# Column means of a weight matrix: four chunk sums side by side on the tensor engine's columns, and one product that adds them

## Chip, cores and metric

The kernel runs on one NeuronCore of a Trainium2 chip. The metric is the device time of one execution in microseconds (us), given as the median of several runs. Where the text names engines: PE is TensorE's matrix multiply, PEld its weight load, DVE is VectorE, ACT is ScalarE, POOL is GpSimd and SP is SyncE, which here only issues DMAs.

## What is computed

Attention with a hashed mask over 4 batches, 8 heads, 768 positions and head size 64, then a Fourier mixing layer and a two-layer MLP on the 4 x 768 x 512 result:

```python
mask = q_bucket[:, :, :, None] == k_bucket[:, :, None, :]     # 6 sign bits of q @ proj, k @ proj
scores = np.where(mask, scale * np.matmul(q, k.transpose(0, 1, 3, 2)), -1000000000.0)
attn = softmax(scores);  x = attn @ v, heads side by side      # (4, 768, 512)
mixed = np.real(np.fft.fft(np.fft.fft(x, axis=1), axis=2))
u = x + mixed
mu = np.mean(u, axis=-1, keepdims=True)
var = np.mean((u - mu) ** 2, axis=-1, keepdims=True)
un = (u - mu) / np.sqrt(var + 1e-06)
ch = np.maximum(un @ w_ch1, 0.0) @ w_ch2                       # 512 -> 2048 -> 512
return (u + ch).astype(np.float32)
```

Subtracting the mean of `u` over its 512 entries before the product with `w_ch1` is the same as subtracting from every column of `w_ch1` its mean over the 512 rows. The kernel does the latter, once, and the change is in how these column means are made. The two weight matrices come in as 64-bit floats and are narrowed to float32 on the core.

## The kernel before

**Stages.** `_main` runs batch by batch. `attention(b)` goes through four pairs of heads (`n`, 0 to 15 over the batches) and six chunks of 128 keys each (`c`). A step is one chunk: `weigh` makes scores for two halves of the queries (two PE groups, `sc`), ACT takes the exponential (`pk`, L860; there are two `pk` buffers), DVE adds the chunks up (`acc`, L944); `values` multiplies the chunk before by v (`oo`, L877). At the end of a pair, in the first step of the next one, `scale` sums over keys with a matrix of ones (`sum`, L897, two groups), and DVE transposes (L901), inverts and multiplies (L904 to L910). `prepare(n + 1)` transposes the next pair's q and k on DVE (L747) and makes their hash bits: for the pairs in `LITE` as `bitsq` and `bitsk` (L776, read by DVE at L778), for later pairs as `bits` (L791), four products of 32 columns each, written to the four groups of 32 partitions of one PSUM tile.

**What runs beside it.** In batch 0 each attention step is followed, in four steps out of five, by one step of `weights1()`: slice `i` of 16 slices of w1 (128 x 512 each, four row chunks `c` for each of four column blocks `f`) is narrowed by `convert(i)`: L631, L635 and L641 on DVE, L639, L646 and L647 on ACT, and a DMA for slice i + 7 issued by POOL. After the fourth slice of block 0, and again of block 512, `average(f)` and `centre(f, ...)` follow: four products with a 128 x 128 matrix `mean` whose entries are 1/512, accumulated in one PSUM tile (`wm`, L654), and four subtractions on DVE that read it from PSUM (L662). Blocks 1024 and 1536 are averaged after the last step of batch 0; ACT copies these two averages to SBUF (`mean`, L1442), and their eight subtractions are written after the second step of batch 1. From batch 1 on, `mix(b - 1)` runs beside attention: the folds (L994 to L1012, DVE), the channel transform (`cs`, L1034), the sequence transform (`A`, `B`, L1063), and the MLP. In batch 0's MLP, `quarters` (L1136 to L1142) makes sums of w1's quarters on DVE in one buffer (`tq`) and stores them to DRAM (`ad`) through the SP queue, where batches 1 to 3 fetch them.

**Order.** Batch 0's attention with `weights1` and the four averages stands in a block that keeps PE, DVE, ACT and POOL in the order in which the code is written (`manual_schedule`). The rest is ordered by a planner, which takes instructions by priority (by default the order in which they are written) and by when it reckons them ready. Every engine then works through its own list in order.

**PSUM.** During batch 0 to 2 `pt` hands out the two banks of the pool `ps_1` in turn; an averaging tile, the two `sum` tiles of `scale` and the bit tiles all go through these two.

Of the kernel before, what the change touches and what calls it, by code (L numbers as in the profile page):

```python
# [11 lines left out]
F32 = mybir.dt.float32  # L12
# [8 lines left out]
P = 128  # L21
B, H, S, D = 4, 8, 768, 64
NBITS = 6
DM = H * D
DFF = 4 * DM
# [5 lines left out]
NDC = DM // P  # L31
GTT = 2
GT = GTT * P
WC = 512
# [445 lines left out]
def _main(  # L480
# [13 lines left out]
    nc = tc.nc  # L494
# [13 lines left out]
    def wt(shape, dtype, tag, name, bufs=2):  # L508
        return work.tile(shape, dtype, tag=tag, name=name, bufs=bufs)
# [4 lines left out]
    def pt(shape, name):  # L514

        turn[0] += 1
        if roomy[0] and turn[0] % 2:
            if turn[0] % 4 == 1:
                return ps_o.tile(shape, F32, tag="o", name=name)
            return ps_sc.tile(shape, F32, tag="sc", name=name)  # L520
        return ps_1.tile(shape, F32, tag="ps", name=name)
# [14 lines left out]
    def load(n, names="qkv", second=nc.sync):  # L536

        b, t = divmod(n, NPAIR)
        for nm in names:
            src = {"q": q, "k": k, "v": v}[nm]
            tag, bufs = ("vn", 2) if nm == "v" else ("qkn", 2)
            tl = wt([P, S], F32, tag, f"{nm}n{n}", bufs)
            nat[nm, n] = tl
            if nm == "v" or n == 0:
                tc_ = tl.rearrange("p (c h d) -> p c h d", c=NT, h=2)
                for h in range(2):  # L550
                    s = src[b, 2 * t + h]
                    s = (
                        s.rearrange("(p c) d -> p c d", c=NT) if nm == "q"
                        else s.rearrange("(c p) d -> p c d", p=P)
                    )
                    (second if h else nc.sync).dma_start(tc_[:, :, h, :], s)
                continue
            for i in range(4):
                s = src[b, 2 * t + i // 2, :, i % 2 * 32 : i % 2 * 32 + 32]
                d = tl[32 * i : 32 * i + 32]  # L560
                if nm == "k":
                    nc.sync.dma_start(
                        d.rearrange("p (j a) -> p j a", a=32),
                        s.rearrange("(j b) a -> b j a", b=32),
                    )
                else:
                    s = s.rearrange("(j b r) a -> r b j a", b=32, r=2)
                    d = d.rearrange("p (r j a) -> r p j a", r=2, a=32)
                    for r in range(2):
                        nc.sync.dma_start(d[r], s[r])  # L570
# [23 lines left out]
    ones = const.tile([P, D], F32, tag="ones", name="ones")  # L594
# [12 lines left out]
    sq = const.tile([P, 2, 2, HALF + 1], F32, tag="sq", name="sq")  # L607
    ch = const.tile([P, 2, 2, DM // 2], F32, tag="ch", name="ch")
    mean = const.tile([P, P], F32, tag="mean", name="mean")
    nc.gpsimd.memset(mean, 1.0 / DM)  # L610
    w1 = const.tile([P, NDC, DFF], F32, tag="w1", name="w1")
    w2 = const.tile([P, NFC, DM], F32, tag="w2", name="w2")

# [35 lines left out]
        )  # L649

    def average(f):
        ps = pt([P, WC], f"wm{f}")
        for c in range(NDC):
            nc.tensor.matmul(  # L654
                ps, mean, w1[:, c, f : f + WC], start=(c == 0), stop=(c == NDC - 1)
            )
        return ps

    def centre(f, avg):
        for c in range(NDC):  # L660
            w = w1[:, c, f : f + WC]
            nc.vector.tensor_tensor(w, w, avg, op=ALU.subtract)  # L662
# [32 lines left out]
    def weights1():  # L695
        slices = [
            (w1[:, c, f : f + WC], moe_w_ch1[c * P : (c + 1) * P, f : f + WC])
            for f in range(0, DFF, WC)
            for c in range(NDC)
        ]  # L700
        zt = wt([P, 3, 2 * WC], F32, "z", "zraw1", 1)
        ft = wt([P, 12, WC], F32, "F", "fraw", 1)
        raws = [zt[:, i] for i in range(3)] + [
            ft[:, i : i + 2].rearrange("p i w -> p (i w)") for i in range(0, 8, 2)
        ]
        arrival = Arrival(slices, raws, 0)
        for i in range(arrival.depth):
            arrival.fetch(i, nc.sync)
            if i == 1:
                load(1)  # L710
        yield
        for i in range(len(slices)):
            arrival.convert(i, ft[:, 8 + i % 4].bitcast(I32))
            yield
            if i % NDC == NDC - 1:


                f = i // NDC * WC
                if f < DFF // 2:
                    centre(f, average(f))  # L720


    xs = {}
# [188 lines left out]
    def attention(b):  # L912
        xs[b] = wt([P, NPAIR, S], F32, "x", f"x{b}")
        pending = []

        def finish():
            n, c, pk, oos, sums = pending.pop(0)
            with behind() if n >= NPAIR and t is not None else nullcontext():
                values(n, c, pk, oos)
            if c == NT - 1:  # L920
                scale(n, oos, sums)

        for t in range(NPAIR):
            n = NPAIR * b + t
            half = fold(b, 0) if t == NPAIR - 1 else iter(())
            if 1 < n + 1 < NPAIR * B:
                load(n + 1)
            ahead = prepare(n + 1) if n + 1 < NPAIR * B else iter(())
            oos = [ps_o.tile([P, 512], F32, tag="o", name=f"oo{n}_{g}") for g in range(2)]
            acc = wt([P, 2, 2, HALF], F32, "t6", f"acc{n}", 2)  # L930
            first = None
            for c in range(NT):
                pk = weigh(n, c)
                new = pk[:, :, :, 0:HALF]
                sums = [acc]
                if c == 0:
                    first = new
                elif c == NT - 1 and b == 0:

                    sums.append(new)  # L940
                else:

                    for g in (0, 1) if b == 0 else (slice(0, 2),):
                        nc.vector.tensor_tensor(  # L944
                            acc[:, g], (first if c == 1 else acc)[:, g], new[:, g],
                            op=ALU.add,
                        )
                while pending:
                    finish()
                pending.append((n, c, pk, oos, sums))  # L950
                if c > 2:
                    next(half, None)
                if c > 0:
                    next(ahead, None)
                yield
        t = None
        while pending:
            finish()
# [459 lines left out]


    other = weights1()  # L1420
    next(other)
    nc.sync.dma_start(ch, cn["ch"].ap())
# [4 lines left out]
    with tc.manual_schedule(engines={ET.PE, ET.DVE, ET.Activation, ET.Pool}):  # L1427
        for _ in prepare(0):
            pass
        roomy[0] = False  # L1430
        for i, _ in enumerate(attention(0)):
            if i % 5 < 4:
                next(other, None)
        for _ in other:
            pass
        pwf = wt([P, 2, P], F32, "t6", "pwf", 2)
        nc.sync.dma_start(pwf, cn["pw"].ap())
        nc.scalar.copy(pw, pwf)
        means = []
        for f in range(DFF // 2, DFF, WC):  # L1440
            means.append((f, wt([P, WC], F32, "u", f"mean{f}", 2)))
            nc.scalar.copy(means[-1][1], average(f))  # L1442
    for b in range(B):
        if b > 0:

# [15 lines left out]
        if b == B - 1:  # L1461
# [7 lines left out]
            ps = pt([1, 3, P], "norms_t")  # L1469
# [25 lines left out]
def kernel(tc, *args):  # L1495

    cn = {n: tc.nc.inline_tensor(a, name="k_" + n) for n, a in _consts().items()}
    with ExitStack() as ctx:
        large = _main(ctx, tc, *args, cn)
    with tc.If(large > 0, preferred_fallthrough_block=False):  # L1500
        _any_scores(tc, *args, cn)
# [34 lines left out]
```

## Time and profile before

| what | value |
|---|---|
| median of 6 runs | 1115.57 us (1111.92 to 1118.81) |
| the profiled execution's own time | 1115.24 us |
| its span in the trace | 1113.5 us |
| mean granted TensorE clock | 0.994 |
| PE busy | 1070.1 us (96%) |
| DVE busy | 779.3 us (70%) |
| ACT busy | 453.5 us (41%) |
| the averages' products (L654) | 32 records, 35.5 to 135.5 us |

The page gives each engine's busy time over one execution. A float32 product shows as two PE records and two weight loads, so 16 products of the averages are 32 records. Successive records on PE overlap in the trace: what a group costs PE is the distance from its first start to the next group's start, not the sum of its durations. A number in brackets behind a row of the timeline is idle time of that engine before it and the instruction that ended it.

### The profile page before, as it was taken

The page shows a single profiled execution, that of the slowest core. Times are in us where ns is not written, and L with a number is a line of the kernel's source. Part 1 is how long each engine was busy: PE and PEld are TensorE (multiplying, and loading weights), DVE is VectorE, ACT ScalarE, POOL GpSimd, SP SyncE. Part 2 cuts the span into 40 slices and gives each one's busy share as a digit, 9 for nine tenths or more (in the row PEclk, how much of TensorE's full clock was granted, in tenths as well). Part 3 has the DMA queues.
Part 4 walks back from the last instruction along what each step waited for, and adds up shares of the span by engine and source line. Part 5 has one row for each costly group of instructions (what it writes and reads, how often), then busy time and mean ns, then how long its engine had stood idle before and what let it go on. Part 6 is the DMA issues. An engine that isn't in the chain of part 4 may idle for free.

```text
span 1113.5 us, 13886 instructions
## 1 busy us (share of the span) xinstructions
PE 1070.1 (96%) x4917; PEld 656.7 (59%) x4917; DVE 779.3 (70%) x1298; ACT 453.5 (41%) x875; POOL 79.5 (7%) x141
## 2 busy tenths in 40 slices
PE   7989998999999999999999999999999999999996
PEld 3434354455845576555664567645674569768675
DVE  5879978639589586985767796884866875644353
ACT  6768445525064224354325522354215422341420
POOL 1000000002110020030000011021000002100000
PEclk9999999999999999999999999999999999999998
DMA  9744544611056144223144234123032205122401
GB/s 227 198 96 100 95 134 141 214 35 26 1 132 209 43 101 141 43 67 82 29 147 94 68 67 165 32 46 95 20 110 71 73 32 170 48 86 73 135 19 41
DMA packets 175566, 103.13 MB, mean 93 GB/s; under 512 B 129408, under 2 KB 162816, under 8 KB 175488
## 3 DMA queue, kind: packets, MB, share of 16 engines
q1 hardware_dynamic: 168400, 83.93, 28.3%
q0 software_dynamic: 5520, 17.83, 5.1%
q8 instruction: 41, 0.67, 0.3%
q10 hardware_dynamic: 1568, 0.39, 0.2%
q14 instruction: 37, 0.30, 0.1%
HBM read 81.14 MB, written 20.97 MB: 92 GB/s over the span
## 4 chain that ended last, share of the span: by engine, by line
PE 63%; DVE 13%; ACT 2%; DMA 2%; issue 2%; DVEq 0%; ACTq 0%
PE o L1219 23%; PE h_p L1348 18%; PE h L1301 6%; PE sc L856 5%; PE oo L877 5%; DVE pk L866 4%; DVE acc L944 2%; PE cs L1034 2%; DMA zraw<-in_moe_w_ch_dram 2%; PE A L1063 1%; PE B L1063 1%; DVE x L1077 1%; PE sum L897 1%; ACT pk L860 1%; PE bits L791 1%
## 5 line engine op out<-in xcount | busy, mean ns | idle before, releaser
L1219 PE MATMUL o<-w,h 128*128 128x256 f32 x1152 | 258.9, 382 | 0.1
L1219 PEld LDWEIGHTS o<-w,h 128*128 128x128 f32 x1152 | 216.9, 190 | 42.4 <-issue 4.7
L860 ACT ACTIVATE pk<-sc 128x768 f32<-128x768 f32 x192 | 148.2, 808 | 98.9 <-PE sc L856 69.9
L866 DVE SCALAR_TENSOR_TENSOR pk<-qb,kb,pk 128x768 f32<-128x768 bf16 x132 | 128.7, 1013 | 64.7 <-ACT pk L860 61.9
L877 PE MATMUL oo<-pk,vn 128*64 128x385 f32 (+1 forms) x768 | 150.1, 500 | 5.2 <-DVE pk L866 2.6
L856 PE MATMUL sc<-qt,kt 64*128 64x384 f32 x768 | 152.5, 502 | 0.2 <-ACT pk L860 0.2
L1348 PE MATMUL h_p<-x,w 128*128 128x384 f32 x384 | 139.0, 493 | 1.4 <-ACT h L1389 1.4
L944 DVE TENSOR_TENSOR acc<-acc,pk 128x1536 f32<-128x1536 f32 (+1 forms) x72 | 105.7, 1482 | 1.6 <-ACT pk L860 1.1
L1348 PE MATMUL h_p<-w 128*128 128x384 f32 x288 | 106.0, 491 | 0.7 <-ACT u L1090 0.7
L1348 PEld LDWEIGHTS h_p<-x,w 128*128 128x128 f32 x384 | 70.5, 190 | 57.6 <-ACT h L1389 5.1
L877 PEld LDWEIGHTS oo<-pk,vn 128*64 128x64 f32 x768 | 48.5, 136 | 93.9 <-issue 74.0
L856 PEld LDWEIGHTS sc<-qt,kt 64*128 64x128 f32 x768 | 66.5, 186 | 47.4 <-issue 24.3
L1301 PE MATMUL h<-x,w 128*128 128x384 f32 x256 | 88.1, 499 | 2.6 <-ACT h L1305 2.6
L1348 PEld LDWEIGHTS h_p<-w 128*128 128x128 f32 x288 | 53.3, 190 | 40.9 <-ACT w L1397 3.3
L1301 PEld LDWEIGHTS h<-x,w 128*128 128x128 f32 x256 | 48.3, 193 | 40.1 <-ACT h L1305 4.1
L1249 ACT COPY tq<-o 128x256 f32<-128x256 f32 x24 | 8.9, 372 | 114.9 <-PE o L1219 114.9
L1231 DVE SCALAR_TENSOR_TENSOR w<-o,rs,w 128x256 f32<-128x256 f32 x56 | 26.8, 480 | 40.7 <-PE o L1219 40.7
L1219 PE MATMUL o<-w 128*128 128x256 f32 x192 | 46.1, 383 | 4.0 <-DVE w L1231 2.4
L972 POOL DMA_DIRECT2D out_dram<-w x30 | 16.3, 546 | 430.3 <-issue 309.0
L1219 PEld LDWEIGHTS o<-w 128*128 128x128 f32 x192 | 35.9, 190 | 11.3 <-DVE w L1231 4.5
L1238 ACT COPY tq<-o 128x256 f32<-128x256 f32 x24 | 8.9, 371 | 74.8 <-PE o L1219 74.8
L1265 DVE TENSOR_TENSOR tq<-tq,o 128x256 f32<-128x256 f32 x24 | 10.1, 421 | 38.1 <-PE o L1219 38.1
(158 smaller groups left out, 1278.2 us busy)
## 6 DMA issues: line engine op xcount, KB each, us to landing
w<-ad SPq DMA_DIRECT2D x168, 128.0 KB, 2.0
w<-bd SPq DMA_DIRECT2D x42, 512.0 KB, 4.5
zraw<-in_moe_w_ch_dram POOLq DMA_DIRECT2D x21, 512.0 KB, 4.6
bd<-w SPq DMA_DIRECT2D x14, 512.0 KB, 5.0
vn<-in_v_dram SPq DMA_DIRECT2D x32, 192.0 KB, 3.3
qn<-in_q_dram SPq DMA_DIRECT2D x120, 48.0 KB, 2.3
kn<-in_k_dram SPq DMA_DIRECT2D x60, 96.0 KB, 3.2
ad<-tq SPq DMA_DIRECT2D x8, 512.0 KB, 3.9
```

The source lines that it names most:

```text
L856: last[0] = nc.tensor.matmul(ps[:, h, 0:HALF], kt[rows, ks], qt[rows, qs], start=kb is not None, stop=True,)
L860: nc.scalar.activation(pk[:, g, :, 0:HALF], ps[:, :, 0:HALF], AF.Exp, scale=SCALE)
L866: nc.vector.scalar_tensor_tensor(w, qb[:, h].rearrange("p (g s) -> p g s", g=2), kb[:, h, c : c + 1], w, op0=ALU.is_equal, op1=ALU.mult,)
L877: nc.tensor.matmul(oos[g][h * D : (h + 1) * D, 0:w], nat["v", n][:, (2 * c + h) * D : (2 * c + h + 1) * D], pk[:, g, h, 0:w], start=(c == ...
L944: nc.vector.tensor_tensor(acc[:, g], (first if c == 1 else acc)[:, g], new[:, g], op=ALU.add,)
L972: (nc.sync if b == B - 1 else nc.gpsimd).dma_start(out[b, s0 : s0 + 2 * w - 1 : 2, cols], src[at : at + w, cols])
L1034: nc.tensor.matmul(ps[:, pc + 2 * lo : pc + 2 * hi - 1 : 2], z[:, cp, pc, par, t * P : (t + 1) * P], ch[:, cp, pc, lo:hi], start=(cp == 0) ...
L1063: nc.tensor.matmul(ps[:, cols], F[:, par, k, t, j * P : (j + 1) * P], sq[:, t, k, cols], start=(t == 0), stop=(t == 1),)
L1219: nc.tensor.matmul(ps, a[:, r], right7[i][:, r], start=start and r == 0, stop=r == HF // 2 - 1, skip_group_check=not start,)
L1231: nc.vector.scalar_tensor_tensor(t[:, cols], src, r, t[:, cols], op0=ALU.mult, op1=ALU.add)
L1301: nc.tensor.matmul(ps, w1[:, c, fc * P : (fc + 1) * P], x[:, c, cols], start=(c == 0), stop=(c == NDC - 1),)
L1348: nc.tensor.matmul(ps, ring[n % NR][:, k], right[i][:, k], start=start and k == 0, stop=k == 1, skip_group_check=not start,)
```

## The change

`average` becomes a generator of two halves. The first half makes, for each of the four row chunks, one product with 32 columns of ones, each into another group of 32 partitions of one PSUM tile (`ws`): partitions 32c to 32c + 31 then all hold chunk c's column sums. ACT copies that tile to SBUF (`part`). The second half is a single product of `part` with the 128 x 128 matrix, whose entries become 1/(32 x 512), into another PSUM tile (`wm`): it adds the four chunks and spreads the mean over all partitions.

In `weights1` the second half and the four subtractions no longer stand ahead of the next slice's `convert`, but one step of attention later, behind that `convert` and ahead of the following one. For the last two blocks both first halves are written first, then both second halves, each with its copy.

```diff
-    nc.gpsimd.memset(mean, 1.0 / DM)
+    nc.gpsimd.memset(mean, 1.0 / (32 * DM))
...
     def average(f):
-        ps = pt([P, WC], f"wm{f}")
+
+
+        ps = pt([P, WC], f"ws{f}")
         for c in range(NDC):
             nc.tensor.matmul(
-                ps, mean, w1[:, c, f : f + WC], start=(c == 0), stop=(c == NDC - 1)
+                ps[32 * c : 32 * c + 32, :], ones[:, 0:32], w1[:, c, f : f + WC],
+                start=True, stop=True,
             )
-        return ps
+        part = wt([P, WC], F32, "u", f"part{f}", 2)
+        nc.scalar.copy(part, ps)
+        yield
+        ps = pt([P, WC], f"wm{f}")
+        nc.tensor.matmul(ps, mean, part, start=True, stop=True)
+        yield ps
...
         yield
+        half = None
         for i in range(len(slices)):
             arrival.convert(i, ft[:, 8 + i % 4].bitcast(I32))
             yield
+            if half:
+                centre(half[0], next(half[1]))
+                half = None
             if i % NDC == NDC - 1:
...
                 f = i // NDC * WC
                 if f < DFF // 2:
-                    centre(f, average(f))
+                    half = f, average(f)
+                    next(half[1])
...
         means = []
-        for f in range(DFF // 2, DFF, WC):
+        late = [(f, average(f)) for f in range(DFF // 2, DFF, WC)]
+        for _, avg in late:
+            next(avg)
+        for f, avg in late:
             means.append((f, wt([P, WC], F32, "u", f"mean{f}", 2)))
-            nc.scalar.copy(means[-1][1], average(f))
+            nc.scalar.copy(means[-1][1], next(avg))
```

## The prediction

> **What bounds the kernel now.** I read the page first, then the busy time by stage, then the averages' tile and the bits' tile, then the timeline around each average.
>
> ```profile
> PE 1070.1 (96%) x4917; PEld 656.7 (59%) x4917; DVE 779.3 (70%) x1298; ACT 453.5 (41%) x875; POOL 79.5 (7%) x141
> ...
> 40.00:64.00 24.00, 20.99 (x120) 8.87 (x116) 22.20 (x35) 18.96 (x33) 2.11 (x4) 1.00 0.74 151
> ...
> 100.00:128.00 28.00, 26.04 (x152) 11.12 (x148) 25.72 (x46) 15.35 (x28) 0.12 (x1) 1.00 0.52 123
> 128.00:136.00 8.00, 8.00 (x26) 3.38 (x24) 7.24 (x13) 1.96 (x4) 0.00 (x0) 1.00 0.79 131
> ```
>
> Over the span PE is the bound (96%). But the averages lie in the first 136 us, and there the table by stage (columns: window, its length, busy us of PE, PEld, DVE, ACT, POOL, clock, DMA share, GB/s) shows DVE about as full as PE: 22.2 against 21.0 of 24 us, 25.7 against 26.0 of 28, and 7.2 of the 8 us in which PE does little but the last two averages. What PE saves here is worth something only where DVE, working through its list in order, waits for PE.
>
> ```profile
> L654 PE MATMUL wm<-w,mean x32: 592/592/697, 35.5 to 134.9; 128*128 128x512 f32 x32
> L1442 ACT COPY mean<-wm x2: 585/585/585, 132.1 to 135.6; 128x512 f32<-128x512 f32 x2
> ...
> 149.42 0.52 PE L791 MATMUL bits<-qt,pj 128*32 128x384 f32 x2
> 149.44 0.52 PE L791 MATMUL bits<-kt,pj 128*32 128x384 f32 x2
> 149.77 0.49 PE L791 MATMUL bits<-qt,pj 128*32 128x384 f32 x2
> 149.78 0.49 PE L791 MATMUL bits<-kt,pj 128*32 128x384 f32 x2
> 150.21 2.96 PE L1034 MATMUL cs<-ch,z 128*128 128x256 f32 x16
> ```
>
> The `bits` lines are the form that the change brings: four products of 32 columns in one tile. Their eight records start as two bunches 0.34 us apart, and the next group starts 0.79 us after the first: four products run for the price of one.
>
> ```profile
> 35.49 3.70 PE L654 MATMUL wm<-w,mean 128*128 128x512 f32 x8
> 39.12 0.34 PE L849 MATMUL sc<-qkb 64*128 64x384 bf16 x2
> 39.23 2.48 DVE L662 TENSOR_TENSOR w<-w,wm 128x512 f32<-128x512 f32 x4 [3.42 <-PE wm L654]
> ...
> 64.82 3.70 PE L654 MATMUL wm<-w,mean 128*128 128x512 f32 x8 [1.65 <-DVE qkb L778]
> 68.56 2.48 DVE L662 TENSOR_TENSOR w<-w,wm 128x512 f32<-128x512 f32 x4 [3.27 <-PE wm L654]
> 76.23 0.58 DVE L901 STREAM_TRANSPOSE rt<-sum 128x384 f32<-128x384 f32 x1 [1.41 <-PE sum L897]
> ...
> 128.39 7.13 PE L654 MATMUL wm<-w,mean 128*128 128x512 f32 x16
> 137.25 0.69 DVE L662 TENSOR_TENSOR w<-w,mean 128x512 f32<-128x512 f32 x1
> 138.99 4.31 DVE L662 TENSOR_TENSOR w<-w,mean 128x512 f32<-128x512 f32 x7
> 143.54 1.77 DVE L944 TENSOR_TENSOR acc<-pk,pk 128x1536 f32<-128x1536 f32 x1
> 145.40 1.51 ACT L860 ACTIVATE pk<-sc 128x768 f32<-128x768 f32 x2 [4.69 <-DVE acc L944]
> 146.26 0.34 PE L849 MATMUL sc<-qkb 64*128 64x384 bf16 x2 [1.42 <-ACT pk L860]
> ```
>
> At the first two averages DVE stands idle 3.4 and 3.3 us for PE. At the last two it doesn't: its list runs without a break from 129 us to 145.3, ends with the eight subtractions and then the `acc` that frees a `pk` buffer, and the chain DVE, ACT, PE at 143.5, 145.4 and 146.3 is what ends PE's wait.
>
> **What the change costs and saves on PE.** One average now: 35.49 to 39.12, 3.63 us (eight records 0.43 apart, 3.43, and 0.20 to the next group). The chunk sums: two bunches of 512 columns, 0.86, plus the 0.15 by which the `bits` group exceeds its two passes of 0.32: 1.02. The adding product: two records and the same end, 0.86 + 0.20 = 1.06. So a pair is 2.08, saving 1.55 each. The last two run without a change between them: 1.92 for both sums, then 0.86 twice and 0.20, 3.84 against 7.06 (128.39 to 135.45), 3.2 saved. All four: 6.3 us, 0.57% of the time. Were this all on the path, 1109.2.
>
> Here the Trainium skill speaks against the row. "TensorE: Matmul & The Clock Gate", in "Measured speedup vs the span model", puts column packing about level with row packing, where four tiles gave 3.07 times, not four. That would make the sums 3.63 / 3.07 = 1.18 us instead of 1.02, 0.16 more per average. The `bits` row gives (4 x 0.645 + 0.15) / 0.79 = 3.5 times in this kernel, so I take 1.02; by the page the total below loses about 0.3 us.
>
> **Block 0 (35.5 us).** Order after: sums, ACT copy, slice 4's `convert`; the next step of attention (`sc`, `oo`, `sum`); then the adding product, subtractions, slice 5. PE: sums 35.49 to 36.5, `sc` and `oo` 2.6 us earlier than now, `sum` at 39.65 (42.18). ACT: the copy sits in its queue ahead of slice 4's L639, which now starts at 34.87 in the shadow of the averaging. It waits for PE until 36.6, takes 0.585, and slice 4 (2.26 us, 34.87 to 37.13) ends at 39.4; the first `pk` behind it starts at 39.4 instead of 40.15. DVE: slice 4 goes first, held to 37.8 by ACT's L639, done at 38.5; then it waits for `sum` until 41.2 (1.55 after its start, as now). L901 to L910 take 4.43 (43.73 to 48.16), the four subtractions 2.40 (39.23 to 41.63): slice 5 starts at 41.2 + 6.83 = 48.03, now 48.16. DVE's wait for the average has turned into a wait for `sum`, and the subtractions, which used to be done ahead of it, come behind it. `acc` at 50.05, for which ACT already waits, comes 0.1 us earlier. Gain 0.1; by the page's 1.18, about nothing.
>
> **Block 512 (64.8).** The sums wait for the same bank of PSUM, until 64.82. They end at 65.84 (68.45 now). ACT's copy ends at 66.5; slice 8, now done by 61.6, is queued behind it and ends at 68.7, so `pk` starts at 68.7 (69.48). DVE does slice 8 by 67.8, waits for the adding product (PE: `sc` and `oo` 65.84 to 69.0, then the product; DVE sees it 1.17 after its start, as 68.56 is 0.31 behind the last record's pitch), subtracts 70.17 to 72.57, does slice 9 by 74.5. PE reaches `sum` at 69.0 + 1.06 + 3.06 = 73.1 (74.68). So L901 starts at 74.7 where it starts at 76.23: 1.5 gained. From there to 128 DVE has only short waits (0.36, 0.71, 0.22), all for groups that shift with it, so the 1.5 stays.
>
> **Blocks 1024 and 1536 (128.4).** PE saves 3.2. DVE's 15 us of work from 128.5 to 143.5 (L901, L747, L906, L910, the fold, eight subtractions) waits for none of it: the second mean is copied at 136.1 now and the subtractions begin at 137.25. With that list as it is, PE is earlier at its first scores and then waits that much longer at 146.26. Between 0 and 3.2; nearest is DVE's full row, and I take 0.5, for work of PE's that can slip forward (`cs`).
>
> **The rest.** The four copies, 4 x 0.585 = 2.3 us, are ACT's; counted above for blocks 0 and 512, and in the last step the first copy (to 1.64 after the start) is covered by the second group of sums (to 1.92). Without that cover the adding product would wait 0.7. The page "TensorEngine Tiling (Array Packing)", under "PSUM Bottleneck", warns that tiling speeds up PE but not the emptying of PSUM: fully exposed, an average would be 1.02 + 0.05 + 0.585 + 1.06 = 2.7, saving 0.9 instead of 1.55; the block 512 trace has another `sc` and `oo` (3.1 us) over it, so it costs nothing there. The 32-column weight loads (106 ns against 190) lie beside products. The PSUM turn: four tiles more, an even number, so each later tile keeps its bank; the added `sum`/`wm` sharing makes `wm` of block 0 wait for L901 (41.8), before PE gets there. `part` shares two buffers with the means, again an even number. No DMA is added; POOL's fetches for slices 11 and 15 go out about 4 us earlier, and SP's queue has nothing new. The memset's value costs nothing.
>
> Sum: 0.1 + 1.5 + 0.5 = 2.1. The profiled execution took 1115.24 (span 1113.5 and 1.7 around it), 0.3 below the median of 1115.57; taken from the median, 1113.5. A measurement of this kernel can tell about 0.3% (3.3 us) from no change, so this is within it.
>
> **Rivals.**
> - *The late saving passes through.* The `acc` at 143.54 is written ahead of the eight subtractions, but its `pk` was not yet reckoned ready when DVE's list was made (it ended at 140.7). With scores 3.2 us earlier the planner can put `acc` ahead of them, and PE's wait ends earlier by up to the 3.2. Gain 0.1 + 1.5 + 3.2 = 4.8: 1110.8. Against it: what the planner assumes for the sums isn't in the trace.
> - *Slower: an `acc` behind `quarters`.* L1136 writes `tq` and must wait for the store of its last contents: DVE waits 0.69 at 149.39 and 2.97 at 155.92 for that DMA. If the planner reckons five products for an average where there were four, it sees PE later, and an `acc` falls behind such an L1136. At the first, `acc` starts at 149.39 + 4 x 0.43 = 151.1 instead of 143.54, 7.6 later; `cs` groups brought forward (150.21 to 153.09 and 1.16) cover 4. Net 3.6 a time; twice it is 7.2 - 1.6 = 5.6 slower, 1121.2. It decides from 5 us of such waits on. For it: everything after 136 us is ordered by the planner, whose start is moved; against it, no line shows that the order changes.
> - *The order falls out better* in the same way: below 1109.
> - *Not side by side.* If the four sums ran one after another, an average costs 3.63 + 1.06 and about 3.6 us are lost: 1119. The `bits` rows speak against it.
>
> **How the numbers follow.** The sum: 0.33 (same 0.22, faster 0.09, slower 0.02), its own range 1110.8 to 1115.2. Late saving passes: 0.25 (faster 0.23, same 0.02). `acc` behind `quarters`, or another order that costs as much: 0.29 (slower 0.28, same 0.01). Better order: 0.09, faster. One after another: 0.04, slower. Together faster 0.41, same 0.25, slower 0.34. The range leaves out half of the better orders and the tail of the worse: 1107 to 1123.
>
> **What would show it.** `ws` as two bunches, next group about 1.0 us after its start; DVE's wait at block 0 put down to `sum`; slice 5 on DVE near 48.0; L901 after block 512 near 74.7; the scores after the last averages near 130.6; `acc` near 142. Wrong if `acc` stands ahead of the subtractions (then faster), or behind an L1136 with a DMA wait (then slower), or if stages after 200 us differ in length at all.

## Result, and the profile after

| | before | after |
|---|---|---|
| median, same chip | 1115.18 us of 39 runs (1111.92 to 1118.81) | 1111.09 us of 18 runs (1109.03 to 1116.05) |
| ratio of after to before | | 0.9967, 95% interval 0.9957 to 0.9977 |
| profiled execution, own time | 1115.24 us | 1113.72 us |
| its span; mean granted clock | 1113.5 us; 0.994 | 1111.9 us; 0.993 |

By the ratio the change is worth 3.7 us (2.6 to 4.8): more than the forecast 2.1, in the same direction, inside the range. The profiled execution of after lies 2.6 us above after's median, so its end tells less than half of the gain; where in the span time is won and lost has to be read with that in mind.

The lines that answer to those shown of before follow. Line numbers have moved: the chunk sums are L656, their copy L661, the adding product L664, the subtractions L670, `rt` L914, `acc` L957, `pk` L873, the scores L862, `tq` L1149 to L1152 with its store at L1155. First the page's busy row, then the answers for the three tiles of an average.

```profile
PE 1065.6 (96%) x4925; PEld 652.4 (59%) x4925; DVE 778.5 (70%) x1298; ACT 456.0 (41%) x879; POOL 79.2 (7%) x141
```

```profile
L656 PE MATMUL ws<-w,ones x32: 592/592/617, 34.8 to 127.2; 128*32 128x512 f32 x32
L661 ACT COPY part<-ws x4: 586/586/588, 35.9 to 128.0; 128x512 f32<-128x512 f32 x4
...
L664 PE MATMUL wm<-part,mean x8: 592/592/697, 41.6 to 130.1; 128*128 128x512 f32 x8
```

The number of records hardly moves (32 became 40), and each is as long as before, 592 ns. What changed is that four of them run at once, which only the timeline shows. It gives start, length, engine, line, and in brackets the idle time before and what ended it:

```profile
34.80 1.07 PE L656 MATMUL ws<-w,ones 128*32 128x512 f32 x8
35.80 0.34 PE L862 MATMUL sc<-qkb 64*128 64x384 bf16 x2
40.41 0.58 DVE L914 STREAM_TRANSPOSE rt<-sum 128x384 f32<-128x384 f32 x1 [2.58 <-PE sum L910]
44.83 2.48 DVE L670 TENSOR_TENSOR w<-w,wm 128x512 f32<-128x512 f32 x4
47.22 0.42 DVE L631 TENSOR_SCALAR w<-fraw 128x512 int32<-128x512 int32 x1
...
63.90 1.07 PE L656 MATMUL ws<-w,ones 128*32 128x512 f32 x8 [1.65 <-DVE qkb L791]
68.06 1.13 PE L664 MATMUL wm<-part,mean 128*128 128x512 f32 x2
69.12 0.34 PE L862 MATMUL sc<-qkb 64*128 64x384 bf16 x2
69.23 2.48 DVE L670 TENSOR_TENSOR w<-w,wm 128x512 f32<-128x512 f32 x4 [2.30 <-PE wm L664]
73.73 0.58 DVE L914 STREAM_TRANSPOSE rt<-sum 128x384 f32<-128x384 f32 x1
...
125.89 1.92 PE L656 MATMUL ws<-w,ones 128*32 128x512 f32 x16
127.75 0.34 PE L862 MATMUL sc<-qkb 64*128 64x384 bf16 x2
128.66 1.98 PE L664 MATMUL wm<-part,mean 128*128 128x512 f32 x4
130.57 0.34 PE L862 MATMUL sc<-qkb 64*128 64x384 bf16 x2
...
136.50 1.30 DVE L670 TENSOR_TENSOR w<-w,mean 128x512 f32<-128x512 f32 x2
137.71 1.76 DVE L957 TENSOR_TENSOR acc<-pk,pk 128x1536 f32<-128x1536 f32 x1
139.37 3.10 DVE L670 TENSOR_TENSOR w<-w,mean 128x512 f32<-128x512 f32 x5
140.42 0.34 PE L862 MATMUL sc<-qkb 64*128 64x384 bf16 x2 [1.27 <-ACT pk L873]
```

Three things are to be seen. The four sums take 1.00 us to the next group (34.80 to 35.80). At block 0 DVE no longer waits 3.42 us for the average but 2.58 for `sum`. And in the last part `acc` (137.71) has moved in front of five of the eight subtractions; in before it stood behind all of them.

To follow the gain I take the start of one instruction in before minus its start in the other trace: the lead. Every trace has its own offset at 29.4 us, before any average has run: the first microseconds differ by up to 3 us over all traces of this study. What counts is how a column changes downwards. In us; the kernels other than after are those of the experiments below.

| instruction, its start in before | after | after again | last two only | acc last | both | tq first | tq first again | before again |
|---|---|---|---|---|---|---|---|---|
| `oo`, 29.4 | 0.75 | 0.92 | 0.85 | -0.33 | 1.43 | 0.82 | 0.19 | 0.05 |
| `oo`, 124.7 | 2.50 | 2.75 | 0.86 | 1.49 | 3.25 | 2.65 | 2.01 | 0.06 |
| `oo`, 148.0 | 5.84 | 6.09 | 4.21 | 0.24 | 2.23 | 5.98 | 5.35 | 0.07 |
| `oo`, 229.4 | 0.92 | 0.94 | 2.29 | 2.11 | 1.78 | 5.71 | 5.48 | -3.32 |
| `oo`, 316.3 | 0.94 | 0.96 | 2.31 | 2.13 | 1.79 | 5.72 | 5.50 | -3.30 |
| `oo`, 354.7 | 1.50 | 2.95 | 2.48 | 2.67 | 3.45 | 8.27 | 8.30 | -1.51 |
| last `o`, 1103.1 | 1.66 | 3.16 | 2.69 | 2.88 | 3.43 | 8.23 | 8.28 | -1.53 |

So in after 1.75 us come from the first two averages (0.75 to 2.50) and 3.3 from the last two (to 5.84 at 148 us). Then 4.9 are gone by 229 us. One place where time goes is the stretch in which `tq` is stored and reloaded; before first, then after:

```profile
155.92 0.42 DVE L1136 TENSOR_TENSOR tq<-w 128x256 f32<-128x256 f32 x1 [2.97 <-DMA ad<-tq]
157.05 0.42 DVE L1139 TENSOR_TENSOR tq<-w,tq 128x256 f32<-128x256 f32 x1
160.42 0.43 DVE L1136 TENSOR_TENSOR tq<-w 128x256 f32<-128x256 f32 x1 [0.41 <-DMA ad<-tq]
```

```profile
157.57 1.56 POOL L685 DMA_DIRECT2D zraw<-in_moe_w_ch_dram  x3 [51.58 <-ACT F L1060]
157.81 0.42 DVE L1152 TENSOR_TENSOR tq<-w,tq 128x256 f32<-128x256 f32 x1
158.26 0.36 SPq L1155 DMA_DIRECT2D ad<-tq  x1
...
166.40 0.42 DVE L1149 TENSOR_TENSOR tq<-w 128x256 f32<-128x256 f32 x1 [3.71 <-DMA ad<-tq]
```

In after the third quarter is finished at 157.81, 0.76 us later than in before in spite of a lead of four to five: an `acc` stands ahead of its last step. Its store (512 KB) goes out at 158.26, just behind three loads of 512 KB each on POOL's queue (157.57). The chain of waits gives this store 8.12 us, and 3.12 to the one that left at 151.04. The fourth quarter reuses the buffer and so starts at 166.40 where before had it at 160.42. In before it is the fourth quarter's store that leaves with these loads (162.00); it takes 5.67 us, and `tq` is not written again before 317 us.

This is a part of the loss, not all of it: the lead is 4.26 at 156 us and 3.48 at 166, and the rest goes between 166 and 202 us. Its size also depends on the trace that it is counted against. Against the second profile of before (last column) after's lead is 5.77 at 148 us and 4.24 at 229, so only 1.5 us are given back.

### The profile page after: what moved, and what is told of

Its sections match the earlier page's. It is cut to its first block, busy times and chain, and to the rows that moved or that the text cites. A ratio compares the mean times of both kernels' runs of the same rounds, so it can differ in the third digit from the quotient of the medians.

```text
span 1111.9 us, 13908 instructions
## 1 busy us (share of the span) xinstructions
PE 1065.6 (96%) x4925; PEld 652.4 (59%) x4925; DVE 778.5 (70%) x1298; ACT 456.0 (41%) x879; POOL 79.2 (7%) x141
## 4 chain that ended last, share of the span: by engine, by line
PE 68%; DVE 20%; DMA 4%; ACT 3%; issue 2%; SPq 1%; DVEq 0%; ACTq 0%
PE o L1232 23%; PE h_p L1361 18%; PE oo L890 6%; PE sc L869 6%; PE h L1314 6%; DVE acc L957 4%; DVE pk L879 4%; DMA zraw<-in_moe_w_ch_dram 2%; PE cs L1047 2%; PE sum L910 2%; PE A L1076 1%; ACT pk L873 1%; DVE x L1090 1%; DMA ad<-tq 1%; PE B L1076 1%
## 5 line engine op out<-in xcount | busy, mean ns | idle before, releaser
L873 ACT ACTIVATE pk<-sc 128x768 f32<-128x768 f32 x192 | 148.1, 807 | 90.3 <-PE sc L869 60.3
L957 DVE TENSOR_TENSOR acc<-acc,pk 128x1536 f32<-128x1536 f32 (+1 forms) x72 | 105.7, 1482 | 0.5
```

The lines of the kernel that those rows point to most:

```text
L873: nc.scalar.activation(pk[:, g, :, 0:HALF], ps[:, :, 0:HALF], AF.Exp, scale=SCALE)
L957: nc.vector.tensor_tensor(acc[:, g], (first if c == 1 else acc)[:, g], new[:, g], op=ALU.add,)
```

## The experiments

Ratios are against before, run beside the kernel on the same chip, each with its 95% interval.

**Only the first two averages changed.** Blocks 1024 and 1536 keep the four accumulated products. `mean` stays 1/512, and the sums use a tile of 1/32 in place of the ones; the instructions are the same.

```diff
+    part32 = const.tile([P, 32], F32, tag="part32", name="part32")
+    nc.gpsimd.memset(part32, 1.0 / 32)
...
-                    centre(f, average(f))
+                    half = f, average(f)
+                    next(half[1])
...
-            nc.scalar.copy(means[-1][1], average(f))
+            nc.scalar.copy(means[-1][1], whole(f))
```

> Blocks 0 and 512 in the new form, blocks 1024 and 1536 in the old one (four accumulated products each). Main theory (the gain has two parts: block 512 gives 1.5 us because DVE waits for PE there, the last two give the rest through the place of acc in DVE's list): L901 after block 512 about 1.6 us earlier than before when the start of the trace is aligned, acc behind the eight subtractions as before, about 1.5 us faster in all (1113.6), ratio near 0.9987. Rival (PE's saving is what counts, 1.55 us per average wherever it lies): about 3 us faster, 0.9973. Second rival (the stage from 150 to 200 us, which waits for DMAs, swallows what comes before it): no change.

Measured: 1113.45 against 1114.68 us, ratio 0.9983 (0.9974 to 0.9992), 1.9 us faster (0.9 to 2.9). In its trace block 512 wins 1.58 us (the lead of `acc` goes from -1.98 to -0.40), from there to 145 us the lead stays flat, and `acc` stands where it did in before, behind the subtractions. The predicted 1.5 for block 512 holds, place and size.

**Only the last two averages changed.** The complement: `whole` in `weights1`, the two halves after batch 0.

```diff
-                    centre(f, average(f))
+                    centre(f, whole(f))
...
-        for f in range(DFF // 2, DFF, WC):
+        late = [(f, average(f)) for f in range(DFF // 2, DFF, WC)]
+        for _, avg in late:
+            next(avg)
+        for f, avg in late:
```

> Blocks 1024 and 1536 in the new form, blocks 0 and 512 in the old one. Main theory: the scores after the averages start about 3.3 us earlier, acc stands ahead of five of the subtractions and starts some 3.3 us earlier; 2 to 2.6 us faster in the end (1112.6 to 1113.2), since the stage to 200 us gives part of it back. Rival of the prediction (DVE's full list hides it): within 0.5 us of before. Rival (all of PE's saving arrives): 3.2 us faster, 1112.0.

Measured: 1113.26 against 1114.68, ratio 0.9987 (0.9977 to 0.9998), 1.45 us faster (0.2 to 2.6). The trace wins nothing to 125 us and 3.35 to 148 (table), with `acc` at 139.34 ahead of five subtractions, as in after. 1.9 of these are given back by 229. The two parts make 3.35, close to the 3.7 of the whole; the whole run once more on this chip, which follows, came out at 5.0 (3.1 to 6.9).

**After once more.** The same kernel, to see what repeats.

> The changed kernel as it is, once more, for a second profile. Main theory: 0.9967 again; up to 145 us the lead over before is the same as in the first profile (2.5, then 5.8 us, start not aligned), and between 150 and 200 us it shrinks by another amount than the 5.8 to 0.9 us of the first profile, because there the tq store and the w2 loads set the pace and their landing times vary. Rival (the order after the averages loses a fixed amount): the lead at 205 us is 0.9 us again.

Measured: 1110.6 us, ratio 0.9955 (0.9938 to 0.9972). The same gains (1.83 and 3.34) and the same giving back (5.15 by 229) stand in its trace, counted against the same profile of before. The main theory, that another amount would be lost, fell. What does not repeat is 316 to 355 us: 0.56 won in one execution and 1.99 in the other.

**`acc` behind all eight subtractions.** After, with the second chunk's `acc` held back until the last subtraction has been issued. For that the subtractions are written one step of attention earlier.

```diff
-            nc.vector.tensor_tensor(w, w, avg, op=ALU.subtract)
+            centred[0] = nc.vector.tensor_tensor(w, w, avg, op=ALU.subtract)
...
+                        with tc.issue_after(centred[0].ins) if (n, c) == (4, 1) else nullcontext():
...
-                if b == 1 and i == 2:
+                if b == 1 and i == 1:
```

> The changed kernel, but DVE's list is held to the order of before at this place: the acc of the second chunk of batch 1 is kept behind all eight subtractions. Main theory (the place of acc makes the late saving worth something): acc starts 3 us later than in the changed kernel, PE waits for it as long as it is early, and of the 3.2 us at most 0.5 is left: about 1113.3, ratio 0.998. Rival (PE's earlier scores count by themselves, since PE fills the wait with other products): as the changed kernel, 0.9967. Second rival (what is won here is lost to the DMA waits by 200 us anyway): as the changed kernel too, with the lead at 145 us smaller and at 205 us the same.

Measured: 1110.05 against 1114.68, ratio 0.9945 (0.9927 to 0.9963). In its timeline:

```profile
141.73 1.75 DVE L960 TENSOR_TENSOR acc<-pk,pk 128x1536 f32<-128x1536 f32 x1
...
144.43 0.50 PE L864 MATMUL sc<-qkb 64*128 64x384 bf16 x2 [4.27 <-ACT pk L875]
```

`acc` is back at the end of the list, PE waits 4.27 us for the `pk` behind it (1.27 in after), and the lead falls from 4.7 at 142 us to 0.24 at 148. So the place of `acc` decides whether the late saving is still there at 148 us. But the whole time did not get worse, and the theory's 0.998 fell: the lead is 2.1 at 229. A delay put in at 145 us was taken off again. DVE's waits for the `tq` store between 140 and 205 us sum to 3.0 us here, to 8.6 in after and to 4.1 in before; that they are the reason isn't shown. That the total is no worse than after's (0.9955 on this chip) I can't explain; the execution that was profiled lies 2.3 us above this kernel's median.

**`acc` put first, PE left alone.** The counterpart, made in before: the order changed without a saving on PE.

```diff
-                        nc.vector.tensor_tensor(
+                        added[0] = nc.vector.tensor_tensor(
...
-                    for f, avg in means:
-                        centre(f, avg)
+                    with tc.issue_after(added[0].ins):
+                        for f, avg in means:
+                            centre(f, avg)
```

> The kernel before with its old averages; only DVE's list is changed: the acc of the second chunk of batch 1 is put ahead of all eight subtractions. PE reaches the scores no earlier. Main theory: its pk ends at 140.7 us, so acc starts near 140.7 instead of 143.5 and PE's wait at 146.3 ends up to 2.8 us earlier; DVE stands idle some 2 us for it; 1 to 2.5 us faster (about 1113.5), so that half of the late gain is order and not PE time. Rival (without PE's saving the order is worth nothing): within 0.5 us of before.

Measured: 1113.99 against 1115.01, ratio 0.9989 (0.9972 to 1.0005): not told apart from before. The trace is 2.0 us behind from 34 us on, has won 1.5 of that at 148 us, and is 4.8 behind at 229. The order alone does win time at 145 us, less than half of the 3.3; what it is worth in the end stays open.

**No step of attention between the halves.** After, with the second half and the subtractions at once for blocks 0 and 512.

```diff
-                    half = f, average(f)
-                    next(half[1])
+                    avg = average(f)
+                    next(avg)
+                    centre(f, next(avg))
```

> The changed kernel, but for blocks 0 and 512 the second half and the subtractions follow the first half at once, ahead of the next slice's convert, as before. PE waits for ACT's copy in each (sums 1.0, copy 0.6 and its hand-over, product 1.06: 2.75 us against 3.63). Main theory ([...] a fully exposed copy leaves 0.9 us per average): DVE waits about 0.9 us less than before at both blocks and nothing turns into a wait for sum, so block 0 now gains 0.9 where the changed kernel gains 0.2, and block 512 gains 0.9 where it gains 1.6: in all as the changed kernel within 0.5 us. Rival (the step between is what makes it pay): 1.5 us slower than the changed kernel, 1112.6.

Measured: 1112.22 against 1115.01, ratio 0.9973 (0.9958 to 0.9989), not told apart from after. In its timeline:

```profile
36.98 1.07 PE L656 MATMUL ws<-w,ones 128*32 128x512 f32 x8
...
38.80 1.10 PE L664 MATMUL wm<-part,mean 128*128 128x512 f32 x2 [0.75 <-issue]
39.83 0.34 PE L863 MATMUL sc<-qkb 64*128 64x384 bf16 x2
```

Here ACT's copy (38.11 to 38.70) is exposed, though the row puts PE's wait down to its own issue: an average takes 2.85 us (36.98 to 39.83) where with a step between it takes 1.00 + 1.06. Both averages now win the same, 0.78 and 0.81, in place of 0.2 and 1.6. Of the two the sum is 1.6 against 1.8: putting a step between has moved the gain more than added to it.

**One product per average.** Before, with the average of the first row chunk only; the sums over the other three are left out.

```diff
-        for c in range(NDC):
+        for c in range(1):
...
-                ps, mean, w1[:, c, f : f + WC], start=(c == 0), stop=(c == NDC - 1)
+                ps, mean, w1[:, c, f : f + WC], start=True, stop=True
```

> The kernel before with averages of the first of the four row chunks alone: one product in place of four, no copy, no moves; the sum over the other three chunks is left out. It bounds what cheaper averages can give: 1.06 us each (0.86 + 1.06 for the last two), 10.2 us less PE time than before against 6.3 for the change. Main theory (these averages pay only where DVE waits for PE, and from 150 us on DMA waits give part back): 2.6 at each of the first two, 5.1 at the last two, of which about half arrives: 5 to 6 us faster, 1110. Rival (all arrives): 10 us faster, 1105. Second rival (the stage to 200 us caps the gain): no faster than the changed kernel, 1111.

Measured: 1106.05 against 1115.01, ratio 0.992 (0.9899 to 0.9941), 8.9 us (6.6 to 11.3) of the 10.3 that twelve products less take off PE (12 x 0.86). Its trace wins 2.57 at each of the first two averages and 5.5 at the last two, counted at `acc`; at the `oo` of 148 us it has won 9.9 in all. So PE time in the averages is worth nearly its whole length at that point. My working, which called DVE "about as full as PE" and let the last part pass almost nothing, undervalued it; the theory put up for this run was too low as well.

**`tq` stored first.** After, with the store for which `tq` waits issued ahead of the three stores of `w` in each quarter.

```diff
+        nc.sync.dma_start(ad[f, 3:7].rearrange("i p k m -> p i k m"), st)
...
-        nc.sync.dma_start(ad[f, 3:7].rearrange("i p k m -> p i k m"), st)
```

> The changed kernel with one more edit: in quarters the store of tq is issued ahead of the three stores of w1's own blocks, so that it isn't queued behind them on SP. Main theory (between 150 and 200 us the gain is given back where L1149 waits for the tq store, 0.9, 3.9 and 3.7 us in the profile): these waits shrink by about 1.9 us each (three issues of 0.62), and the kernel is 1 to 3 us faster than the changed kernel, about 1109. Rival (the w2 loads, three buffers deep, set the pace there, not tq): within 0.5 us of the changed kernel.

Measured: 1108.53 against 1115.01, ratio 0.9943 (0.9923 to 0.9963). In its timeline:

```profile
155.21 0.42 DVE L1152 TENSOR_TENSOR tq<-w,tq 128x256 f32<-128x256 f32 x1
...
158.59 0.43 DVE L1149 TENSOR_TENSOR tq<-w 128x256 f32<-128x256 f32 x1 [0.33 <-DMA ad<-tq]
```

The third quarter's last step starts at 155.21, ahead of the three loads (157.43), and the fourth quarter at 158.59 after a wait of 0.33, not at 166.40. The two waits before that one are as in after (0.92 and 4.00 against 0.95 and 3.94), so the theory that each would shrink by 1.9 fell. The lead of 5.98 at 148 us falls to 3.13 at 166, much as in after (3.48). Then the two part: it is 6.63 at 181, where after has 2.04, and 5.71 at 229.

The planner's list has changed with the edit: the `acc` that stood ahead of the third quarter's last step now stands behind it. In both traces that quarter's store leaves 0.03 us after the last step has ended (158.23 to 158.26 in after, 155.63 to 155.66 here), so in after it wasn't held up behind the stores of `w`. What lets it leave 2.6 us earlier is the changed list, and not the place of the store.

**The same again**, on another chip.

> The changed kernel with tq stored first, once more. Theory: 0.9943 again, and in the profile the lead over before at 205 us is 5 us or more, with the third quarter closed before the loads of w2 start. Rival (its first result was a lucky set of runs): 0.9967, as the changed kernel, and the lead at 205 us about 1 us.

Measured: 1107.83 against 1114.52, ratio 0.994 (0.9916 to 0.9963), as its theory had it; the lead is 5.35 at 148, 5.48 at 229 and 8.28 at the end. This is the fastest version of the whole computation that ran, 2.6 and 3.3 us under after by medians, though on other chips; each of its two intervals still overlaps after's.

**`tq` stored first in before.** The same two lines moved, without the change.

> The kernel before, with only the tq store issued ahead of the three stores of w1's own blocks. Theory now (the changed kernel gives back its lead because DVE's list there closes the third quarter behind an acc and a cast, so that its store leaves together with the first three loads of w2 and lands 8 us later instead of 3; the kernel before closes it in time): nothing to repair here, within 1 us of before, 0.999 to 1.001. Rival (issuing tq first is worth 2 to 3 us by itself in any order): 0.9975, as much as it gave on the changed kernel.

Measured: 1113.5 against 1114.52, ratio 0.9984 (0.9974 to 0.9994), 1.8 us (0.7 to 2.9). The interval holds the theory's 0.999 as well as the rival's 0.9975. Its trace keeps a lead of 0.57 at 148 us and 0.55 at 229, so in this trace no gain comes in that stretch. With the change's 3.7 it makes 5.5 where 6.4 and 6.7 were measured together, a difference inside the intervals.

**Both: `tq` first and `acc` last.**

> The changed kernel with both edits that looked better: tq stored first, and the acc of the second chunk kept behind the subtractions. Theory (both only avoid the late third quarter, so one is enough): as tq first alone, 0.9943. Rival (the two add up): 0.992.

Measured: 1114.06 against 1114.52, ratio 0.9996 (0.9984 to 1.0008). Both of its theories fell. PE waits 4.29 us for the `pk` behind `acc`, as with `acc` last alone, and the lead goes from 6.45 at 142 us to 2.23 at 148, but this time the total is lost too. From 229 us on the two profiles are alike (2.11 and 1.78, at the end 2.88 and 3.43), but the ratios differ by 0.5%: the profiled execution lies 2.3 us above the median with `acc` last, and 2.4 below it here. No run settles why.

**Before again.**

> The kernel before as it is, for a second profile. Theory (order decides the stage from 150 to 230 us, landing times of the moment the one from 316 to 330): the stage to 230 us takes the same time as in the first profile within 0.8 us, counted from the chunk at 112 us. Rival (that stage varies by several us in a kernel of one order, so that the lead of 0.9 us read at 205 us from single profiles says little): it differs by 2 us or more.

Measured: 1116.47 us, span 1114.7. To 148 us its trace lies on the first one's to 0.1 us. By 229 it is 3.32 behind, by 355 it has 1.8 of that back. The rival holds: the stretch behind the averages varies by 3 us between two executions of one kernel.

## Why the prediction was right, and where it was not

- **The sums and the adding product.** Forecast 1.02 and 1.06; measured 1.00 and 1.06 (68.06 to 69.12). The figure weighed against the row ("TensorE: Matmul & The Clock Gate", "Measured speedup vs the span model", of the Trainium skill), read for column tiles as 3.07 times and 1.18 us, doesn't fit this kernel: 3.63 / 1.00 is 3.6 times. The last two averages take 4.68 us from 125.89 to 130.57, of which 0.91 is a score group that slipped in (127.75 to 128.66); without it 3.77, forecast 3.84.
- **The exposed copy.** The Trainium skill's "TensorEngine Tiling (Array Packing)", "PSUM Bottleneck", warns that PSUM is not emptied any faster, from which the prediction worked out 2.7 us for an average with nothing over ACT's copy. The run agrees: 2.85, with a gain of 0.8 where 0.9 was worked out.
- **Block 0.** Forecast a gain of 0.1 and a wait for the average turned into one for `sum`; measured 0.2 (`acc`, from a lead of 0.75 to 0.94) and a wait of 2.58 for `sum`. Slice 5 was put at 48.0; it starts at 47.22, or 47.97 when the trace's offset of 0.75 is added back. The working put `sum` at 39.65, where 36.51 and its own 3.06 make 39.57; with that its gain comes to the measured 0.2.
- **Block 512.** Forecast 1.5; measured 1.56, and 1.58 when changed with block 0 alone. It stays unchanged to 125 us, as said.
- **Blocks 1024 and 1536: the term that failed.** The prediction held DVE's list fixed ("With that list as it is"), bounded the gain by 0 and 3.2 and took 0.5, since the nearest row was DVE's full one. The list was not fixed: with the earlier scores `acc` stood ahead of five subtractions, and 3.3 us arrived at 148. This is the first rival, mechanism and size, up to that point; the prediction even named `acc` ahead of the subtractions as its refutation, "then faster". That the place of `acc` is worth anything at the end isn't shown: with `acc` held behind, the total was no worse than after's in one kernel and lost in the other.
- **"So the 1.5 stays": right to 148 us, and then not examined.** The sum took any time won by 145 us as won at the end. The traces show a stretch with waits for DMA landings from 148 to 229 us. The two profiles of after give back 5 us in it against the first profile of before and under 2 against the second, and before alone varies by 3. In the total the late part is worth 1.45 us (0.2 to 2.6), between the 0.5 taken and the 3.2 of the rival; the interval holds the 0.5 too. So 2.1 became 3.7: 1.9 where 1.6 was forecast, and 1.45 where 0.5 was. That the two totals lie so near each other is in part luck: at 148 us the change had won 5.1 (0.75 to 5.84), 3.0 more than forecast, and what came off behind that point the prediction didn't have.
- **A sign that decides nothing.** The prediction called itself wrong if stages after 200 us differ in length. They do (0.56 and 1.99 won from 316 to 355 us), but the second profile of before wins 1.8 there as well.
- **The slower rival** (an `acc` behind a quarter that waits for its store) has its like in the trace, in another guise: a quarter behind an `acc`, whose late store then leaves with three loads. What it costs in the end isn't told apart from the 3 us by which the stretch varies; the total is faster all the same.

## What to carry to other kernels

A saving on a full engine is worth what the engines that wait for it can use; but where a planner orders the work behind, the saving also changes the order, so a full list on the other engine is no reason to take the gain near its lower bound. Follow a lead instruction by instruction past the next stretch in which engines wait for DMA landings before counting it, and leave the verdict to medians: here two profiles of one kernel differ by 3 us over such a stretch. Where a buffer is waited for, look at when its store leaves and what leaves with it.

## What the runs showed of the hardware

- A 512 KB store that left 0.69 us behind the first of three 512 KB loads from another queue took 8.12 us by the chain of waits, 7.42 in after again; one that left at 151.04, clear of them, took 3.12. A store of the same size at 216.91 us in after took 8.05 without these three loads, so they are not the only thing that makes one slow.
- In the table by stage of after the granted TensorE clock falls to 0.59 between 52 and 56 us; in after again it is 0.70, in one trace of `tq` first 0.60 and in the other 1.00, in before 1.00. PE's lead in after falls by 2.9 us there (2.26 at 49.8 us, -0.67 at 58.4) and is back at 73.3 (2.50); in the trace of `tq` first whose clock stays at 1.00 it falls by 1.3, so 1.6 go with the lower clock. DVE's `acc` keeps its lead through it (0.94 at 50 us, 0.92 at 63), so nothing of this is lost. What brings the dip on wasn't tried: between 48 and 52 us PE is busy for 2.0 us in the traces with the dip (3.35 in before), but also in the trace of `tq` first without it.
- Before anything that was changed has run, at 29 us, the traces already differ by up to 2.9 us (1.43 ahead of before with both `tq` first and `acc` last, 1.49 behind it without a step between).
